# A fused attention and two expert layers on one core: weight slots, residues and the beginning rearranged

## The chip, the core and the metric

The kernel runs on one core of a Trainium2 chip. The engines named are TensorE (PE in the rows; PEld its weight loads), VectorE (DVE), ScalarE (ACT), GpSimd (POOL) and SyncE (SP), which issues nearly all DMAs. The metric is device time in microseconds; lower is better. Times are from one launch of the whole program.

## The reference

Attention over 2 batches of 8 heads, 768 positions of 64 values, in which a score counts only where the 6-bit hash of query and key agree; then two layers of 1536 tokens, 512 wide, 2048 in the middle.

```python
q_bits = einsum(q, proj) > 0 ; k_bits = einsum(k, proj) > 0     # 6 bits
mask = q_bucket == k_bucket
scores = where(mask, q @ k.T / 8, -1e9)
attn = softmax(scores) ; out = attn @ v                          # per head
x = heads side by side                                           # 1536 x 512
h = x @ w_in ;  g = h * tanh(softplus(h)) ;  x = g @ w_out       # layer 1
h = x @ w_in2 ; g = P(h) / (Q(|h|) + 1e-6) ; out = g @ w_out2    # layer 2, P cubic, Q quadratic
```

The weights arrive as 64-bit floats. Matmuls run on 32-bit floats rounded for TensorE, so each operand is split into a rounded part (`hi`) and a residue (`lo`), and a product is three matmuls: hi·hi, hi·lo and lo·hi.

## The kernel before

**Attention.** The order of the work is written by hand: a table `order` (line 510) gives each operation its step, six steps for a head, and `slot_ops` emits the operations of a step in the table's order. Every engine works through its own queue in that order. In a step of head h TensorE computes the scores `sp` of one block of 128 keys (`st`, line 346) and the matmuls `mp` of one block of a later head (`smax`, 313); VectorE reduces `mp` to its maxima `m` (line 324), ScalarE takes the exponential `e` of `sp` (358). `sp`, `mp` and a small tile of `vsum` share one pool of three PSUM tiles, so a new tile waits for the `e` or `m` that reads an older one. Other steps add `pv` and `dn`, the products of `e` with the values and with ones (two blocks at once in step 5, the sixth step), and `codes`, the hash matmuls `cp`. `cp` and `dn` take turns in a single PSUM bank, which `code_k` (VectorE, 297) and `code_q` (ScalarE, 306) must have read before it comes free.

For each head, `hi` (ScalarE) rounds key and query into `qB`, `lo` takes the residue `qX`: on GpSimd (line 67), for head 0 on VectorE (line 70). SP then moves rows between tiles: `move_k` (230), `move_x` (236), `move_h` (240). `code_q` writes rows of `qB` that `move_k` reads. `fin_a` turns six maxima into a row (`smt`, then `stt`, line 333), and `fin_b` (339) writes it into `qB` by two DMAs from SP and two from GpSimd.

A list `start` (574) gives the first operations by hand, up to the scores of head 0.

**Weights.** A layer has 16 slots (128 columns of `w_in`, 128 rows of `w_out`, each as hi and lo). During attention, ten slots of layer 1 are loaded in halves (`ring_load`) and converted from 64-bit to 32-bit by three VectorE operations (lines 100, 103, 106; "bits"). Slots 0 to 4 are split into hi and lo on GpSimd (a few residues on VectorE) and stored to DRAM (`ring_split`), then loaded into their tiles (`first`); slots 5 to 9 are stored as 32-bit floats. Tiles 0 to 2 of the weights' pool also hold the raw heads that `load` fetches.

**Layers.** `moe` runs iterations i, one slot and one block of 512 tokens each. An iteration issues `gl` (VectorE's residue of the activation of i-1, in `back`), 12 matmuls `h` (`gemm1`), the activation on ScalarE (`front`), and 12 matmuls `y` of i-1 (`gemm2`), whose last four need `gl`. Beside the first block, slots 5 to 9 are loaded as floats and split, and slots 10 to 15 are converted from the 64-bit source in four pieces each through a ring of five tiles: `direct_load`, `direct_bits` in one iteration, `direct_hi` and `direct_lo` in the next. `tail` (593) emits what is left of attention's last heads in iterations 1, 2 and 4.

Of the kernel before, what the change touches and what calls it, by code (L numbers as in the profile page):

```python
# [9 lines left out]
F32 = mybir.dt.float32  # L10
# [10 lines left out]
NF = DFF // 128  # L21
# [6 lines left out]
NBITS = 6  # L28
EARLY, FIRST = 5, (84, 68, 76, 52, 60)
SPLIT1, HERE1, W_AT, W_LEAD = 5, 10, (3, 9, 15, 17, 21), 4  # L30
DVE_LO = (("lo", 0),)
ENG = dict(
    lo="pp", hi="aa", xhi="a", xlo="dd", whi="pppp", wlo="pdpp",
)
C_AT = 16
ROW, TINY = 31, 2.0 ** -60
C1_AT = 2, 14
RING, EP, GB = (2, 5), 4, 2
# [6 lines left out]
def attention_moe_moe(ctx: ExitStack, tc: tile.TileContext, kq, v, proj2, cst, eye, w1, w2, ab, out):  # L45
# [115 lines left out]
    def attention(actx, tctx):  # L161
# [22 lines left out]
        VF = [v_p.tile([128, NC, 2, D], F32, tag=f"vf{i}", name=f"vf{i}") for i in range(2)]  # L184
        ones = v_p.tile([128, 32], F32, tag="ones", name="ones")

        def memsets():
            nc.gpsimd.memset(cs_t, 0.0)
# [6 lines left out]
            nc.gpsimd.memset(ones, 1.0)  # L195
            nc.gpsimd.memset(bias[:, 1:2], 1.000001)
# [73 lines left out]
        def qhalf(t, a):  # L270
            return t[:, a * HALF:(a + 1) * HALF]
# [15 lines left out]
        def codes(h):  # L287
            if not 0 <= h < B * H:
                return
            ct[h] = pvp.tile([128, 512], F32, tag="dn", name="cp")  # L290
            both(ct[h], p_raw, raws[h], start=True, stop=True)

        def code_k(h):
            if not 0 <= h < B * H:
                return
            for a in range(2):
                nc.vector.tensor_scalar(  # L297
                    out=qhalf(KK[h % 4][0:32, 0], a), in0=ct[h][64 * a:64 * a + 32, 0:HALF],
                    scalar1=cs_t[:, 1:2], scalar2=cs_t[:, 2:3], op0=ALU.is_gt, op1=ALU.mult,
                )  # L300

        def code_q(h):
            if not 0 <= h < B * H:
                return
            for a in range(2):
                nc.scalar.activation(
                    out=qhalf(qB[h % 4], a)[0:32], in_=ct[h][64 * a + 32:64 * a + 64, 0:HALF],
                    func=ACT.Sign, bias=cs_t[:, 0:1],
                )
# [164 lines left out]
        nh = B * H  # L474
        parts = [(f, s) for f in range(HERE1 if wide64 else 0) for s in range(PARTS[0])]
        jobs = {}

        def ring_out(l, f, s):
            (ring_split if f < SPLIT1 else ring_store)(l, f, s)

# [4 lines left out]
        for n, p in enumerate(parts):  # L485
            i = n // 5 * 24 + W_AT[n % 5]
            for fn, d in ((ring_load, -W_LEAD), (convert, 0), (ring_out, 1)):
                jobs.setdefault(max(0, i + d), []).append((fn, p))
# [8 lines left out]
        def first(f, n):  # L497
            if wide64:
# [33 lines left out]
            ("xlo", xlo, 24, 0),
            ("vred", vred, -5, 0),
            ("move_x", move_x, -14, 1),
            ("move_h", move_h, -12, 1),
            ("load", load, -31, 1),
# [7 lines left out]
        for name, fn, at, per in order:  # L544
# [29 lines left out]
        start = (
            ("load", 0), ("get", 0), ("get", 1), ("hi", 0), ("codes", 0), ("khi", 0, 0), ("lo", 0), ("load", 1),
            ("code_q", 0), ("code_k", 0), ("khi", 0, 1), ("get", 2), ("move_x", 0), ("smax", 0, 0), ("hi", 1),
            ("smax", 0, 1), ("move_k", 1), ("load", 2), ("lo", 1), ("smax", 0, 2), ("codes", 1), ("move_h", 0),
            ("smax", 0, 3), ("smax", 0, 4), ("smax", 0, 5), ("fin_a", 0), ("fin_b", 0), ("code_k", 1), ("code_q", 1),
            ("load_v", 0), ("move_x", 1), ("load", 3), ("hi", 2), ("move_k", 2), ("smax", 1, 0), ("coef",),
            ("move_h", 1), ("smax", 1, 1),  # L580
        )
# [17 lines left out]
    def moe(mctx, tctx, tail):  # L599
# [114 lines left out]
        def run():  # L714
# [72 lines left out]
            for i in range(-5, len(seq) + 5):  # L787
# [99 lines left out]
```

## Time and profile before

| | us |
|---|---|
| median of 3 runs | 808.4 (806.15 to 809.41) |
| the profiled execution, its own time | 807.36 |
| its span, first to last instruction | 805.3 |
| PE busy | 772.7 (96%) |
| DVE busy | 593.8 (74%) |
| ACT busy | 422.4 (52%) |
| POOL busy | 83.2 (10%) |

All times in rows count from the first instruction of the span. A row of the timeline gives start, duration, engine, line, operation, out<-in with shapes, and how many alike were merged; in brackets the engine's idle time ahead of it and what ended it. PE's duration of a matmul includes the way through its pipeline, so that neighbours overlap. The first `h` of the layers starts at 276.1 us.

### The profile page before, as it was taken

Reading aid. Unit: us, or ns where it says so; the run is one execution under the profiler, and the core shown is the slowest. Engines: PE = TensorE matmul, PEld = TensorE weight load, DVE = VectorE, ACT = ScalarE, POOL = GpSimd, SP = SyncE. Lnnn points to the kernel's source line nnn. Section 1 sums busy time; section 2 is a strip of 40 time slices with the busy share of each in tenths; the row PEclk is TensorE's granted clock in tenths of the full one; section 3 lists DMA queues with packets and bytes.
Section 4 is the critical chain, followed back from the end, with each engine's and each line's share of the span. In section 5 each row is a group of like instructions: output and inputs, shape, how many; then the busy total and the mean of one; then the engine's idle time right before and its main releaser. Section 6 shows DMA issues by size and latency. Waiting matters only on the chain.

```text
span 805.3 us, 10855 instructions
## 1 busy us (share of the span) xinstructions
PE 772.7 (96%) x3744; PEld 571.0 (71%) x3744; DVE 593.8 (74%) x1067; ACT 422.4 (52%) x682; POOL 83.2 (10%) x104
## 2 busy tenths in 40 slices
PE   4799999999999999999999999999999999999997
PEld 2455455555555587888888888887888888888886
DVE  5667878878766367656554667739998988888885
ACT  3345454655555554323122324358787777677664
POOL 3332442531221000000000000000000000000000
PEclk8899999999999999999999999999999999999999
DMA  4757466766765462334454487730000100001001
GB/s 112 211 162 200 147 171 197 211 167 191 223 182 145 123 209 79 105 105 150 157 168 141 138 261 256 221 115 2 1 1 0 53 1 0 1 15 39 0 1 52
DMA packets 60629, 94.91 MB, mean 118 GB/s; under 512 B 20896, under 2 KB 29088, under 8 KB 60576
## 3 DMA queue, kind: packets, MB, share of 16 engines
q1 hardware_dynamic: 59552, 94.21, 39.6%
q8 instruction: 29, 0.48, 0.2%
q14 instruction: 24, 0.20, 0.1%
q0 software_dynamic: 1024, 0.03, 0.1%
HBM read 62.43 MB, written 19.45 MB: 102 GB/s over the span
## 4 chain that ended last, share of the span: by engine, by line
PE 82%; DVE 9%; DMA 5%; ACT 2%; issue 1%; SPq 1%; DVEq 0%; ACTq 0%
PE h L632 30%; PE y L652 16%; PE y L650 14%; PE pv L276 7%; PE sp L353 6%; PE dn L379 4%; PE mp L320 4%; DVE m L324 3%; DMA r<-w 2%; DMA kk<-qX 1%; DVE w L70 1%; DVE t L103 1%; DMA kk<-qB 1%; DVE kk L297 1%; DVE r L106 1%
## 5 line engine op out<-in xcount | busy, mean ns | idle before, releaser
L632 PE MATMUL h<-xh,w 128*128 128x512 f32 x768 | 204.9, 389 | 0.0
L632 PEld LDWEIGHTS h<-xh,w 128*128 128x128 f32 x768 | 144.1, 188 | 30.6 <-issue 0.6
L324 DVE TENSOR_REDUCE m<-mp 128x1 f32<-128x768 f32 x96 | 90.7, 952 | 44.8 <-PE mp L320 44.4
L70 DVE TENSOR_TENSOR gl<-ep,gh 128x512 fp32r<-128x512 f32 x96 | 65.9, 687 | 64.9 <-ACT ep L676 64.2
L358 ACT ACTIVATE e<-sp 128x768 f32<-128x768 f32 x96 | 76.0, 810 | 65.1 <-PE sp L353 63.8
L675 ACT ACTIVATE gh<-h 128x512 fp32r<-128x512 f32 x48 | 28.7, 598 | 147.6 <-PE h L632 138.8
L632 PE MATMUL h<-xl,w 128*128 128x512 f32 x384 | 102.6, 389 | 0.0
L652 PE MATMUL y<-w,gh 128*128 128x512 f32 x384 | 96.3, 389 | 0.0
L650 PE MATMUL y<-gh,w 128*128 128x512 f32 x384 | 94.8, 389 | 0.0
L632 PEld LDWEIGHTS h<-xl,w 128*128 128x128 f32 x384 | 72.1, 188 | 15.0
L650 PEld LDWEIGHTS y<-gh,w 128*128 128x128 f32 x384 | 72.1, 188 | 15.0
L652 PEld LDWEIGHTS y<-w,gh 128*128 128x128 f32 x384 | 72.1, 188 | 15.0
L320 PE MATMUL mp<-kk,qB 128*128 128x384 f32 x192 | 54.7, 374 | 22.8 <-DVE m L324 11.7
L276 PE MATMUL pv<-e,vf 128*64 128x384 f32 x384 | 73.8, 506 | 0.0
L320 PEld LDWEIGHTS mp<-kk,qB 128*128 128x128 f32 x192 | 34.8, 199 | 33.2 <-DVE m L324 16.7
L353 PE MATMUL sp<-qB,kk 128*128 128x384 f32 x192 | 55.8, 371 | 0.6 <-ACT e L358 0.6
L682 ACT ACTIVATE ep<-h 128x512 f32<-128x512 f32 x48 | 28.6, 595 | 52.4 <-PE h L632 52.4
L353 PEld LDWEIGHTS sp<-qB,kk 128*128 128x128 f32 x192 | 31.2, 190 | 33.9 <-issue 17.2
L106 DVE SCALAR_TENSOR_TENSOR r<-r,t 128x256 int32<-128x256 int32 (+1 forms) x108 | 51.2, 474 | 4.6 <-DMA w<-r 0.5
L103 DVE SCALAR_TENSOR_TENSOR t<-r,t 128x256 int32<-128x256 int32 (+1 forms) x108 | 51.7, 479 | 3.7
L652 PE MATMUL y<-w,gl 128*128 128x512 f32 x192 | 53.3, 392 | 0.5 <-DVE gl L70 0.4
L684 DVE TENSOR_TENSOR n<-n,ep 128x512 f32<-128x512 f32 x48 | 33.1, 690 | 26.8 <-ACT n L683 26.8
(72 smaller groups left out, 1037.8 us busy)
## 6 DMA issues: line engine op xcount, KB each, us to landing
r<-w SPq DMA_DIRECT2D x88, 256.0 KB
w<-w SPq DMA_DIRECT2D x21, 512.0 KB
r<-w SPq DMA_DIRECT2D x20, 512.0 KB
w<-r SPq DMA_DIRECT2D x64, 128.0 KB
w<-r SPq DMA_DIRECT2D x30, 256.0 KB
kq<-kq SPq DMA_DIRECT2D x16, 384.0 KB
kk<-qB SPq DMA_DIRECT2D x15, 384.0 KB
w<-w SPq DMA_DIRECT2D x20, 256.0 KB
```

The source lines that it names most:

```text
L70: nc.vector.tensor_tensor(out=o, in0=i, in1=f32(h), op=ALU.subtract)
L103: lambda: nc.vector.scalar_tensor_tensor(out=t, in0=r[:, :, 1], scalar=-0x40000000, in1=t, op0=ALU.bitwise_and, op1=ALU.bitwise_or),
L106: lambda: nc.vector.scalar_tensor_tensor(out=o, in0=r[:, :, 0], scalar=29, in1=t, op0=ALU.logical_shift_right, op1=ALU.bitwise_or),
L276: nc.tensor.matmul(out=o[64 * a:64 * a + 64, 0:HALF], lhsT=w, rhs=qhalf(x, a), start=start, stop=stop)
L320: nc.tensor.matmul(out=p[:, a, 0:HALF], lhsT=qB[h % 4][:, c * 128:(c + 1) * 128], rhs=qhalf(KK[h % 4][:, 0], a), start=True, stop=True,)
L324: nc.vector.tensor_reduce(out=mt[h][:, c:c + 1], in_=halves(p), op=ALU.max, axis=AX.XY)
L353: nc.tensor.matmul(out=p[:, a, 0:HALF], lhsT=kk[:, c * 128:(c + 1) * 128], rhs=qq[:, a * HALF:(a + 1) * HALF], start=(i == 0), stop=(i == 1),)
L358: nc.scalar.activation(out=wide(e), in_=halves(p), func=ACT.Exp, scale=1.0 / D ** 0.5)
L632: nc.tensor.matmul(out=p, lhsT=w[:, c * 128:(c + 1) * 128], rhs=x[:, c, :], start=(n == 0), stop=(n == 11))
L650: nc.tensor.matmul(out=y[m], lhsT=w[:, DM + m * 128:DM + (m + 1) * 128], rhs=g, **s)
L652: nc.tensor.matmul(out=y[m], lhsT=g[:, m * 128:(m + 1) * 128], rhs=w[:, DM:2 * DM], **s)
L684: nc.vector.tensor_tensor(out=v_, in0=v_, in1=u, op=ALU.mult)
```

## The change

- Seven weight slots (`EARLY = 7`) are converted during attention, one half in each head, at steps 7, 13, 19, ... Slots 0 to 2 (`SHARED = 3`) go through DRAM as before; slots 3 to 6 are split by GpSimd straight into their tiles (`slot_split`). Nothing is stored as 32-bit floats for layer 1 any more. All residues of weights in attention are GpSimd's.
- Nine slots, 7 to 15, are converted beside layer 1's first block in four pieces each, from iteration 1 on (it was six, from iteration 2); hi and residue are taken in the iteration of the bits.
- The residues `lo` of all heads are VectorE's.
- Other steps: `hi`, `move_k`, `lo`, `code_q`, `norm`, `xlo`, `vred`, `move_x`, `move_h`; the maxima of heads 1 and 2 are spread over later steps.
- Another `start`: three loads of heads first; the codes of head 0 are computed twice, into a second PSUM tile for ScalarE; 28 calls of `warm`, a matmul of ones by ones of 128 columns into that tile; the maxima of head 0 are taken between residues of heads 1 and 2.

```diff
-EARLY, FIRST = 5, (84, 68, 76, 52, 60)
-SPLIT1, HERE1, W_AT, W_LEAD = 5, 10, (3, 9, 15, 17, 21), 4
+EARLY, SHARED, FIRST = 7, 3, (78, 66, 72, 60, 60, 60, 60)
+W_AT, W_LEAD = 7, 4
 ENG = dict(
-    lo="pp", hi="aa", xhi="a", xlo="dd", whi="pppp", wlo="pdpp",
+    lo="dd", hi="aa", xhi="a", xlo="dd", whi="pppp", wlo="pppp",
 )
-C1_AT = 2, 14
+C1_AT = 1, 14
...
+    def slot_split(l, f, s):
+        w = raw.pop((l, f, s)).bitcast(F32)[:, 0:CH[l]]
+        if (l, f) not in W:
+            slot(l, f, lambda f: wpool)
+        h = W[l, f][:, 0, part(l, s)]
+        hi_of("whi", f)(h, w)
+        lo_of("wlo", f)(W[l, f][:, 1, part(l, s)], w, h)
...
-            ct[h] = pvp.tile([128, 512], F32, tag="dn", name="cp")
-            both(ct[h], p_raw, raws[h], start=True, stop=True)
+            ct[h] = [pvp.tile([128, 512], F32, tag="dn", name="cp")] * 2
+            if h == 0:
+                ct[h][1] = warm_up[0]
+            for t in ct[h][0:1 + (h == 0)]:
+                both(t, p_raw, raws[h], start=True, stop=True)
+        def warm(n):
+            if not warm_up:
+                warm_up.append(pvp.tile([128, 512], F32, tag="pv", name="wm"))
+            for _ in range(n):
+                nc.tensor.matmul(out=warm_up[0][0:32, HALF:512], lhsT=ones, rhs=wones, start=True, stop=True)
...
-            (ring_split if f < SPLIT1 else ring_store)(l, f, s)
+            ring_split(l, f, s) if f < SHARED else slot_split(l, f, s)
...
-            i = n // 5 * 24 + W_AT[n % 5]
+            i = W_AT + 6 * n
...
-            ("hi", hi, -18, 1),
-            ("move_k", move_k, -17, 1),
-            ("lo", lo, -18, 1),
+            ("hi", hi, -16, 1),
+            ("move_k", move_k, -15, 1),
+            ("lo", lo, -15, 1),
...
-            ("code_q", code_q, -15, 1),
+            ("code_q", code_q, -14, 1),
...
-                todo = [(c // 2 if h == 1 else at + 6 * h + c, (h, c)) for h in range(nh) for c in range(per)]
+                todo = [((at, c - 2, 4 + c)[h] if h < 3 else at + 6 * h + c, (h, c)) for h in range(nh) for c in range(per)]
...
+            ("load", 0), ("get", 0), ("get", 1), ("load", 1), ("load", 2), ("warm", 5), ("hi", 0), ("codes", 0),
+            ("khi", 0, 0), ("lo", 0), ("warm", 5), ("code_k", 0), ("code_q", 0), ("hi", 1), ("khi", 0, 1), ("get", 2),
+            ("move_k", 1), ("lo", 1), ("move_x", 0), ("smax", 0, 0), ("warm", 2), ("smax", 0, 1), ("warm", 2), ("hi", 2),
...
-                        at(i + 1, direct_hi, f, s)
-                        at(i + 1, direct_lo, f, s)
-                        at(spread(n - RING[1], C1_AT, NF - HERE1) + 1 if n >= RING[1] else -1, direct_load, f, s)
+                        at(i, direct_hi, f, s)
+                        at(i, direct_lo, f, s)
+                        at(spread(n - RING[1], C1_AT, NF - EARLY) if n >= RING[1] else -1, direct_load, f, s)
```

SP's queue in the beginning, before. `kk_130<-qB_122` is `move_k` of head 3, the two `qB_120<-stt_118` are `fin_b` of head 1, `kq` the load of a head.

```order
L230 DMA kk_129<-qB_121 64x2x768
L240 DMA qX_124<-qB_120 64x768
L236 DMA kk_129<-qX_125 64x768
L240 DMA qX_125<-qB_121 64x768
L205 DMA kq<-kq 128x768 x2
L119 DMA r<-w 128x1024
L230 DMA kk_130<-qB_122 64x2x768
L339 DMA qB_120<-stt_118 1x6x32 x2
L211 DMA vf_132<-v 128x12x64
```

The same stretch of SP's queue now.

```order
L251 DMA qX_124<-qB_120 64x768
L247 DMA kk_129<-qX_125 64x768
L216 DMA kq<-kq 128x768 x2
L251 DMA qX_125<-qB_121 64x768
L222 DMA vf_132<-v 128x12x64
L362 DMA qB_120<-stt_118 1x6x32 x2
L241 DMA kk_130<-qB_122 64x2x768
L119 DMA r<-w 128x1024
```

`move_k` of head 3 has come from ahead of head 1's `fin_b` to behind it.

VectorE's queue in a head in the middle, before: from a `fin_a` (`smt`, `stt`) on, with a conversion of a half of weights (L100 to L106) behind `code_k` (L297).

```order
L330 TENSOR_SCALAR smt1_116<-m_1004 128x6
L333 STREAM_TRANSPOSE stt1_118<-smt1_116 128x32
L324 TENSOR_REDUCE m_1158<-mp_1191 128x1
L297 TENSOR_SCALAR kk1_128<-cp_1195,cst_114 32x384 x2
L324 TENSOR_REDUCE m_1158<-mp_1211 128x1
L268 TENSOR_SCALAR vsc_1223<-vsp_1220 128x2
L100 TENSOR_SCALAR t_1227<-r_1131 128x512
L103 SCALAR_TENSOR_TENSOR t_1227<-r_1131,t_1227 128x512
L106 SCALAR_TENSOR_TENSOR r_1131<-r_1131,t_1227 128x512
L324 TENSOR_REDUCE m_1158<-mp_1238 128x1
```

The same of VectorE now, for the same head.

```order
L353 TENSOR_SCALAR smt1_116<-m_1018 128x6
L356 STREAM_TRANSPOSE stt1_118<-smt1_116 128x32
L100 TENSOR_SCALAR t_1189<-r_1090 128x512
L103 SCALAR_TENSOR_TENSOR t_1189<-r_1090,t_1189 128x512
L106 SCALAR_TENSOR_TENSOR r_1090<-r_1090,t_1189 128x512
L347 TENSOR_REDUCE m_1165<-mp_1200 128x1
L320 TENSOR_SCALAR kk1_128<-cp_1205,cst_114 32x384 x2
L347 TENSOR_REDUCE m_1165<-mp_1225 128x1
L70 TENSOR_TENSOR qX1_124<-kq_843,qB1_120 128x768
L279 TENSOR_SCALAR vsc_1239<-vsp_1236 128x2
```

The conversion has moved two reductions ahead, and the residue `qX` stands where it was.

VectorE's queue in one iteration of layer 1, before: from one `gl` to the next, two pieces (`r`) and the residues of a slot in floats (`w8`) and of two pieces of the iteration before.

```order
L70 TENSOR_TENSOR gl_2886<-ep_2854,gh_2855 128x512
L100 TENSOR_SCALAR t_2884<-r_2818 128x256
L103 SCALAR_TENSOR_TENSOR t_2884<-r_2818,t_2884 128x256
L106 SCALAR_TENSOR_TENSOR r_2818<-r_2818,t_2884 128x256
L100 TENSOR_SCALAR t_2885<-r_2868 128x256
L103 SCALAR_TENSOR_TENSOR t_2885<-r_2868,t_2885 128x256
L106 SCALAR_TENSOR_TENSOR r_2868<-r_2868,t_2885 128x256
L70 TENSOR_TENSOR w8_2703<-w8_2703 128x512 x2
L70 TENSOR_TENSOR w11_2838<-r_2757,w11_2838 128x256
L70 TENSOR_TENSOR w11_2838<-r_2816,w11_2838 128x256
L70 TENSOR_TENSOR gl_2937<-ep_2905,gh_2906 128x512
```

An iteration of VectorE now, from one `gl` to the next (neither shown): three pieces, bits and residues.

```order
L100 TENSOR_SCALAR t_2725<-r_2648 128x256
L103 SCALAR_TENSOR_TENSOR t_2725<-r_2648,t_2725 128x256
L106 SCALAR_TENSOR_TENSOR r_2648<-r_2648,t_2725 128x256
L100 TENSOR_SCALAR t_2726<-r_2650 128x256
L103 SCALAR_TENSOR_TENSOR t_2726<-r_2650,t_2726 128x256
L106 SCALAR_TENSOR_TENSOR r_2650<-r_2650,t_2726 128x256
L100 TENSOR_SCALAR t_2727<-r_2707 128x256
L103 SCALAR_TENSOR_TENSOR t_2727<-r_2707,t_2727 128x256
L106 SCALAR_TENSOR_TENSOR r_2707<-r_2707,t_2727 128x256
L70 TENSOR_TENSOR w8_2700<-r_2648,w8_2700 128x256
L70 TENSOR_TENSOR w8_2700<-r_2650,w8_2700 128x256
L70 TENSOR_TENSOR w9_2758<-r_2707,w9_2758 128x256
```

The residues of the pieces now belong to the bits of the same iteration.

## Rows read from the trace of the kernel before

**Rows 1.** Stretches: window, PE, PEld, DVE, ACT, POOL busy, clock, DMA share, GB/s.

```profile
20.00:58.00 38.00, 32.34 (x174) 18.18 (x173) 25.38 (x38) 16.05 (x23) 14.95 (x17) 0.93 0.68 181
58.00:276.00 218.00, 207.12 (x1242) 115.23 (x1242) 159.50 (x274) 115.56 (x173) 60.95 (x69) 0.99 0.64 181
```

**Rows 2.** PE's waits: total us, times, longest.

```profile
PE mp L320 <- DVE m L324: 11.7, 12, 1.9
```

**Rows 3.** Timeline of PE: start, duration, operation, idle time ahead.

```profile
4.08 1.55 PE L276 MATMUL cp<-kq,pr 128*64 128x384 f32 x4 [4.08 <-DMA pr<-proj]
...
19.23 0.84 PE L353 MATMUL sp<-qB,kk 128*128 128x384 f32 x2
...
27.48 0.62 PE L320 MATMUL mp<-kk,qB 128*128 128x384 f32 x2 [3.66 <-ACT qB L306]
...
86.88 0.90 PE L320 MATMUL mp<-kk,qB 128*128 128x384 f32 x2 [1.88 <-DVE m L324]
87.72 2.83 PE L276 MATMUL pv<-e,vf 128*64 128x384 f32 x8
...
97.81 0.87 PE L276 MATMUL cp<-kq,pr 128*64 128x384 f32 x4
```

**Rows 4.** Timeline of the beginning: `hi` of head 1, transpose of head 0.

```profile
7.86 0.84 ACT L61 ACTIVATE qB<-kq 128x768 fp32r<-128x768 f32 x1
...
15.54 0.21 DVE L333 STREAM_TRANSPOSE stt<-smt 128x32 f32<-128x32 f32 x1
```

**Rows 5.** Timeline of one head in the middle, all engines.

```profile
124.80 0.51 PE L353 MATMUL sp<-qB,kk 128*128 128x384 f32 x2
...
126.05 1.51 PE L276 MATMUL pv<-e,vf 128*64 128x384 f32 x8
...
129.79 1.55 SPq L339 DMA_DIRECT2D qB<-stt  x2
...
131.52 0.68 SPq L230 DMA_DIRECT2D kk<-qB  x1
...
133.77 0.42 DVE L100 TENSOR_SCALAR t<-r 128x512 int32<-128x512 int32 x1
...
135.36 1.16 ACT L306 ACTIVATE qB<-cp,cst 32x384 fp32r<-32x384 f32 x2 [3.13 <-DMA kk<-qB]
...
135.62 0.95 DVE L324 TENSOR_REDUCE m<-mp 128x1 f32<-128x768 f32 x1
...
136.62 0.62 PE L320 MATMUL mp<-kk,qB 128*128 128x384 f32 x2 [1.08 <-DVE m L324]
```

**Rows 6.** Groups by line: count, busy us, mean ns of one, idle before.

```profile
L70 DVE TENSOR_TENSOR qX<-kq,qB 128x768 fp32r<-128x768 f32 x1 | 1.0, 958 | 4.7 <-ACT qB L61 4.7
...
L426 DVE TENSOR_SCALAR z<-rc 24x32 f32<-24x32 f32 x16 | 6.6, 413 | 0.5
...
L429 DVE TENSOR_SCALAR rc<-rc 24x32 f32<-24x32 f32 x16 | 2.7, 170 | 0.5
...
L67 POOL TENSOR_TENSOR r<-r 128x512 fp32r<-128x512 f32 x8 | 10.3, 1293 | 0.7
```

**Rows 7.** Timeline of VectorE in layer 1, and one wait of PE.

```profile
284.55 0.29 DVE L100 TENSOR_SCALAR t<-r 128x256 int32<-128x256 int32 x1 [0.87 <-DMA r<-w]
...
302.09 0.76 DVE L70 TENSOR_TENSOR w<-r,w 128x256 fp32r<-128x256 f32 x2
302.76 0.68 DVE L70 TENSOR_TENSOR gl<-ep,gh 128x512 fp32r<-128x512 f32 x1
...
304.15 0.42 DVE L106 SCALAR_TENSOR_TENSOR r<-r,t 128x256 int32<-128x256 int32 x1
305.85 0.30 DVE L100 TENSOR_SCALAR t<-r 128x256 int32<-128x256 int32 x1 [1.28 <-DMA r<-w]
...
322.21 1.20 PE L650 MATMUL y<-gl,w 128*128 128x512 f32 x4 [0.49 <-DVE gl L70]
```

**Rows 8.** Chain that ended last, in order of time: start, us, what.

```profile
323.41 2.72 PE h L632 x12
```

More of the change, by code (lines that the diff above doesn't have):

```diff
@@ L185, in attention @@
         ones = v_p.tile([128, 32], F32, tag="ones", name="ones")
+        wones = v_p.tile([128, 128], F32, tag="wones", name="wones")
         def memsets():
+            nc.vector.memset(ones, 1.0)
+            nc.vector.memset(wones, 1.0)
             nc.gpsimd.memset(cs_t, 0.0)
@@ L194, in memsets @@
                 nc.gpsimd.memset(f32(SM[i]), 0.0)
-            nc.gpsimd.memset(ones, 1.0)
             nc.gpsimd.memset(bias[:, 1:2], 1.000001)
@@ L289, in codes @@
                 return
-            ct[h] = pvp.tile([128, 512], F32, tag="dn", name="cp")
-            both(ct[h], p_raw, raws[h], start=True, stop=True)
+            ct[h] = [pvp.tile([128, 512], F32, tag="dn", name="cp")] * 2
[3 more added lines that the diff above has]
+                both(t, p_raw, raws[h], start=True, stop=True)
+        warm_up = []
+        def warm(n):
[3 more added lines that the diff above has]
+                nc.tensor.matmul(out=warm_up[0][0:32, HALF:512], lhsT=ones, rhs=wones, start=True, stop=True)
         def code_k(h):
@@ L297, in code_k @@
                 nc.vector.tensor_scalar(
-                    out=qhalf(KK[h % 4][0:32, 0], a), in0=ct[h][64 * a:64 * a + 32, 0:HALF],
+                    out=qhalf(KK[h % 4][0:32, 0], a), in0=ct[h][0][64 * a:64 * a + 32, 0:HALF],
                     scalar1=cs_t[:, 1:2], scalar2=cs_t[:, 2:3], op0=ALU.is_gt, op1=ALU.mult,
@@ L306, in code_q @@
                 nc.scalar.activation(
-                    out=qhalf(qB[h % 4], a)[0:32], in_=ct[h][64 * a + 32:64 * a + 64, 0:HALF],
+                    out=qhalf(qB[h % 4], a)[0:32], in_=ct[h][1][64 * a + 32:64 * a + 64, 0:HALF],
                     func=ACT.Sign, bias=cs_t[:, 0:1],
@@ L474, in attention @@
         nh = B * H
-        parts = [(f, s) for f in range(HERE1 if wide64 else 0) for s in range(PARTS[0])]
+        parts = [(f, s) for f in range(EARLY if wide64 else 0) for s in range(PARTS[0])]
         jobs = {}
         def ring_out(l, f, s):
-            (ring_split if f < SPLIT1 else ring_store)(l, f, s)
+            ring_split(l, f, s) if f < SHARED else slot_split(l, f, s)
         def convert(l, f, s):
@@ L497, in first @@
         def first(f, n):
-            if wide64:
+            if wide64 and f >= SHARED:
+                pass
+            elif wide64:
                 if n == 0:
@@ L529, in attention @@
             ("spread", spread, 12, 1),
-            ("norm", norm, 22, 0),
+            ("norm", norm, 23, 0),
             ("xhi", xhi, 23, 0),
[L532 to L535, printed above, removed]
+            ("xlo", xlo, 29, 0),
+            ("vred", vred, -6, 0),
+            ("move_x", move_x, -13, 1),
+            ("move_h", move_h, -11, 1),
             ("load", load, -31, 1),
@@ L549, in attention @@
             elif name == "smax":
-                todo = [(c // 2 if h == 1 else at + 6 * h + c, (h, c)) for h in range(nh) for c in range(per)]
+                todo = [((at, c - 2, 4 + c)[h] if h < 3 else at + 6 * h + c, (h, c)) for h in range(nh) for c in range(per)]
             elif name.startswith("fin_"):
-                todo = [(at + 6 * h + (h == 1), (h,)) for h in range(nh)]
+                todo = [((at, 3, 9)[h] if h < 3 else at + 6 * h, (h,)) for h in range(nh)]
             elif per > 0:
@@ L574, in attention @@
         start = (
[L575 to L580, printed above, removed]
+            ("load", 0), ("get", 0), ("get", 1), ("load", 1), ("load", 2), ("warm", 5), ("hi", 0), ("codes", 0),
+            ("khi", 0, 0), ("lo", 0), ("warm", 5), ("code_k", 0), ("code_q", 0), ("hi", 1), ("khi", 0, 1), ("get", 2),
+            ("move_k", 1), ("lo", 1), ("move_x", 0), ("smax", 0, 0), ("warm", 2), ("smax", 0, 1), ("warm", 2), ("hi", 2),
+            ("smax", 0, 2), ("warm", 2), ("move_k", 2), ("lo", 2), ("move_h", 0), ("smax", 0, 3), ("warm", 2),
+            ("smax", 0, 4), ("warm", 2), ("smax", 0, 5), ("codes", 1), ("fin_a", 0), ("fin_b", 0), ("code_q", 1),
+            ("code_k", 1), ("load_v", 0), ("move_x", 1), ("load", 3), ("warm", 8), ("smax", 1, 0), ("smax", 1, 1),
+            ("move_h", 1), ("coef",),
         )
@@ L587, in run @@
             for name, *k in start:
+                if name == "warm":
+                    warm(*k)
+                    continue
                 done.add(("move_k" if name == "khi" else name, tuple(k[:1]) if name == "khi" else tuple(k)))
@@ L761, in run @@
             for f in range(EARLY, NF):
-                if wide64 and f < SPLIT1:
-                    at(-1, slot_both, 0, f, wp)
-                elif wide64 and f >= HERE1:
+                if wide64:
                     for s in range(PARTS[1]):
-                        n = PARTS[1] * (f - HERE1) + s
-                        i = spread(n, C1_AT, NF - HERE1)
+                        n = PARTS[1] * (f - EARLY) + s
+                        i = spread(n, C1_AT, NF - EARLY)
                         at(i, direct_bits, f, s)
-                        at(i + 1, direct_hi, f, s)
-                        at(i + 1, direct_lo, f, s)
-                        at(spread(n - RING[1], C1_AT, NF - HERE1) + 1 if n >= RING[1] else -1, direct_load, f, s)
+                        at(i, direct_hi, f, s)
+                        at(i, direct_lo, f, s)
+                        at(spread(n - RING[1], C1_AT, NF - EARLY) if n >= RING[1] else -1, direct_load, f, s)
                 else:
@@ L796, in run @@
                 for fn, k in now:
-                    if fn in (slot_hi, direct_hi):
+                    if fn is slot_hi:
                         fn(*k)
@@ L805, in run @@
                     o()
+                for fn, k in now:
+                    if fn is direct_hi:
+                        fn(*k)
                 if i >= 0:
```

## The prediction, made before the changed kernel ran

> **What bounds the kernel now.** I read the stretches first, then TensorE's waits, then the timeline of those waits. From 276 us on TensorE has no room: it is the layers' matmuls back to back. The attention ahead of it has room: between 58 and 276 us TensorE is busy 207.12 of 218 us, so 10.88 us idle at a mean granted clock of 0.99, and between 20 and 58 us 32.34 of 38 us, so 5.66 us idle at a mean of 0.93 [rows 1]. Twelve of the waits are for the reduction `m` on VectorE, 11.7 us together [rows 2]. The reader is to see in [rows 3] what such a wait is and what it can drag behind it: the first codes run 1.55 us at 4.08, the same four matmuls 0.87 us at 97.81, nearly twice as long, as the lower of its two levels (1.2 against 2.4 GHz) makes it; after the 1.88 us of idle time at 86.88 the eight `pv` take 2.83 us, and 1.51 us at 126.05 where nothing was idle.
>
> One head in the middle shows the cause [rows 5]. VectorE converts a piece of weights from 133.77 to the reduction at 135.62, 1.85 us; that reduction ends at 136.57 and TensorE, which needs its PSUM tile, sat 1.08 us until 136.62. In the same head ScalarE's `code_q` stands 3.13 us behind the copy `move_k`: issued at 131.52, right behind the 1.55 us of `fin_b` on SP, landed by 135.36, 3.84 us later.
>
> **The middle (58 to 276 us).** The change puts the conversion two steps earlier, into the step with most matmuls after it (`pv`, a third of `dn`), and `code_q` one step later. What VectorE has to do hardly changes: some 12 residues of 0.958 us come to it there [rows 6], 11.5 us, and about five conversions of 1.85 us leave, 9.3 us; so 159.5 us [rows 1] become 162 of 207, 78%. A step of `sp` and `mp` lasts 1.25 us (124.80 to 126.05) [rows 5], with `pv` 1.51 more and with the long `dn` as much again, and a whole head some 15 us, its steps at 0, 1.2, 4.7, 6.7, 9.4 and 10.6. With `sp` and `mp` ahead, 0.95 us each and the other work of the step behind them, the reductions end at 2.1, 3.2, 6.7, 9.1, 11.7 and 13.8 us; a score matmul needs the reduction of two steps before, and those stand at 4.7, 6.7, 9.4, 10.6, 14.7 and 15.9 us. No reduction is last any more. To be gained are the 10.88 us and the slow clock, 0.01 of 207 us, about 1.8: 12.7 us. What is late next is `dn`, since it takes the PSUM bank that `code_q` must have read: by steps `code_q` ends at 12.3 us, in heads with two stores on SP ahead of `move_k` at 12.8, and `dn` stands at 13.3. With a cover of 0.5 to 1 us I leave 1.7 us for heads where SP is later. Bounds: 0 left over, or all 10.88 us in another place. Taken: **11.0 us off**.
>
> A rule of the Trainium skill speaks against this step. The row: `z`, 24x32, takes 413 ns in the mean, the next operation on the same shape 170 [rows 6], so something holds it up. The page "SBUF — State Buffer", section "SBUF: two separate sides", says that VectorE with two SBUF inputs and GpSimd lock one port pair, and the loser waits out the other's whole instruction. The residue has two SBUF inputs and GpSimd's weight residue lasts 1.29 us [rows 6]: by the rule 12 times 1.29 us more, VectorE at 86%, still under TensorE; the sum stays, and the third rival below would have a chance of 0.22 by it.
>
> **The beginning (0 to 58 us).** Before, `stt` of head 0 ends at 15.75 and its scores start at 19.23, 3.5 us later [rows 3, 4]. After: the second copy of the codes ends near 4.08 + 2 x 1.55 = 7.2; `code_q` (1.16) to 8.5, `hi` of head 1 (0.84 [rows 4]) to 9.4; VectorE's residue of head 1 to 10.4, six reductions of 0.95 and the residue of head 2 to 17.0, `fin_a` 0.4: 17.4, and 3.3 to 3.5 us on, 20.7. So 1.5 us later. The warm matmuls add nothing to the path while TensorE waits anyway; without that cover they are 28 calls of 128 columns, about 4 us at the pace of the two 384-column calls (four matmuls) in 0.87 us.
>
> By the Trainium skill, "TensorE: Matmul & The Clock Gate", section "What's actually happening", the engine starts throttled and activity releases it; [rows 3] agree at 4.08. If the first five warm matmuls did it, the codes would save 0.68 us each copy and the sum would be 1.4 us lower; I count nothing, since TensorE is idle again before the codes.
>
> Then two waits arise that were not there. In the rows of order, SP issued `move_k` of head 3 ahead of head 1's `fin_b`, and now behind it, and `code_q` is a step later. From the end of `mp` of the last block of head 1: reduction 0.95, `fin_a` 0.4, `fin_b` 1.55, landing 3.84, `code_q` 1.16, together 7.9 us; TensorE has till `dn` two `pv`, two steps, `vsum`: 1.51 x 2 + 1.25 x 2 + 0.4 = 5.9. So `dn` of head 0 waits 2 us, and 0.4 more as VectorE is late. One head on the same, with a second reduction ahead and no `vsum`: 8.9 against 5.5, 3.4 us. Behind `dn` on TensorE everything stands, as it is in order. A load (head 3) and ScalarE's queue cost another 1.3 us, and after the longer wait the clock falls once, as at 86.88: 1.4 to 1.8 us. Lost: 2.4 + 3.4 + 1.3 + 1.6 = 8.7 us. Before, the same stretch lost 5.66 us and, at clock 0.93, 2.3 us: 8.0, among it the 3.66 us at 27.48 [rows 1, 3]. So 0.7 us and the 1.5 us: 2.2 us; the bounds go from 6 us on (the clock falls three times) to 4 us off (both waits covered). The new waits being worked out and the cover being not, I take **1.5 us on**.
>
> **Layer 1 (from 276 us).** Nine slots of four pieces are converted beside the matmuls, where it was six slots and ten halves of others already in float. A piece costs VectorE 1.2 us of bits (`gl` at 302.76 to the end of bits at 304.57 is 1.81, `gl` 0.61 of it) and 0.36 of residue (two in 0.76) [rows 7]. Three pieces and `gl`: 5.3 us of the 5.44 us that an iteration lasts (two groups of twelve matmuls, 2.72 us each [rows 8]). It fits, without slack. The wait for a load in each iteration, 1.28 us at 305.85 [rows 7], goes: the residue is taken in the same iteration, so that two pieces stand ready instead of one, and the third comes 4 us after its ring tile is free against about 3.7 us that a load needed. But two iterations carry attention's last heads: in the first, `recip` and `xl`, 2.3 us on top, with the first data not there before 5.8 us after the layer starts (it was 8.5, behind a double-size load that is gone [rows 7]); `gl` is then 0.8 us late. In the fifth, norm and `xl` with ScalarE between, 2.5 us less 0.5 of slack: 2.0 us. The 0.49 us at 322.21 [rows 7] was such a wait and goes. Bounds: 0.5 us off if the data come early, 6 us on if the first data come at 8.5 us as before. Taken: **2.3 us on**.
>
> **Sum.** 11.0 - 1.5 - 2.3 = 7.2 us off the profiled execution of 807.36 us (span 805.3 and 2.1 around it): 800.2 us. The median of the runs shown lies 1.0 us above that execution; inside their spread I take a third of it: 800.5 us. Nothing else in the layers moves.
>
> **Rivals.** (1) The beginning works as well: `move_k` lands before `dn` needs it, the clock stays up. For it: matmuls put just where TensorE idled. Against: the order of SP. Then 5.5 us more come off: 795 us. (2) Slower: VectorE bounds layer 1. If the idle time for a load stays, as 1.28 us at 305.85, an iteration needs 5.3 + 1.3 = 6.6 us, 1.15 us over, 15 us in 13 iterations; less the 5 us of slack that `gl` has at the start, but with the two tail iterations on top 15 to 20 us: 813 us or more. It decides from about 1.1 us of idle time for each iteration on. For it: 5.3 of 5.44. Against: two ready pieces in the ring. (3) The change does not do what it says: the wait of each head moves, from `mp` to `dn` or to the residue. Then 10.9 of the 12.7 us stay, and one clock fall less: 808 us. For it: the thin cover at `dn`. Against: the table of steps.
>
> **Chances.** Forecast 0.50 (own range 794 to 806), (1) 0.20, (2) 0.13, (3) 0.17. Less than 0.5%, 4 us, cannot be told from no change on this kernel. Faster than 804.4: 0.42 + 0.20 + 0.02 + 0.03 = 0.67. Same: 0.07 + 0.03 + 0.12 = 0.22; slower: 0.01 + 0.08 + 0.02 = 0.11. The range of 790 to 809 takes in (1) and (3) and leaves (2).
>
> **What would show it.** Middle: no wait for `m` between 60 and 230 us; each head near 15.1 us, 16 before. Beginning: scores of head 0 at 20 to 21 us; two waits of `dn` for `code_q`, 2 to 4 us, near 35 and 52 us. Layer 1: waits for `gl` in the second and fifth iterations, no VectorE wait for loads after the first. I am wrong if TensorE still idles some 0.8 us in each head, or if the layer loses time in every iteration.

## The result: slower, and the profile after

The changed kernel takes 818.05 us in the median (816.0 to 820.27) against 807.7 for the kernel before on the same chip: ratio 1.0133 [1.0114, 1.0152], 10.4 us slower. The forecast was 800.5 us, its range ended at 809. The span of the profiled execution is 817.6 us, 12.3 more than before.

First the waits of TensorE in the changed kernel (total us, times, longest), then those of ScalarE for the copy of k:

```profile
PE dn L402 <- ACT qB L329: 22.0, 11, 4.0
PE y L679 <- DVE gl L70: 1.6, 1, 1.6
PE sp L376 <- DMA qB<-stt: 1.1, 1, 1.1
PE mp L343 <- DVE m L347: 0.4, 1, 0.4
```

```profile
ACT qB L329 <- DMA kk<-qB: 29.6, 9, 4.9
```

The 11.7 us of `mp` for `m` [rows 2] are gone: 0.4. In their place stand 22.0 us of `dn` for `code_q`, 6.0 of them in the beginning (two waits), 16.0 in nine heads of the middle, and behind that wait `code_q`'s own, for `move_k`'s transfer. The same stretches, and TensorE's timeline:

```profile
20.00:58.00 38.00, 32.50 (x161) 19.23 (x161) 24.67 (x39) 14.32 (x20) 9.10 (x14) 0.91 0.53 139
58.00:276.00 218.00, 199.46 (x1182) 111.36 (x1184) 145.63 (x261) 114.74 (x167) 52.35 (x70) 0.98 0.53 141
...
80.90:83.60 2.70, 2.70 (x16) 0.58 (x16) 0.00 (x0) 0.77 (x1) 0.00 (x0) 0.50 0.41 141
```

```profile
21.95 0.59 PE L376 MATMUL sp<-qB,kk 128*128 128x384 f32 x2 [1.07 <-DMA qB<-stt]
...
38.99 2.23 PE L402 MATMUL dn<-e,ones 128*32 128x384 f32 x16 [2.02 <-ACT qB L329]
...
60.54 2.79 PE L402 MATMUL dn<-e,ones 128*32 128x384 f32 x16 [3.97 <-ACT qB L329]
...
69.27 0.87 PE L287 MATMUL cp<-kq,pr 128*64 128x384 f32 x4
...
80.89 2.79 PE L402 MATMUL dn<-e,ones 128*32 128x384 f32 x16 [3.66 <-ACT qB L329]
...
157.97 0.87 PE L287 MATMUL cp<-kq,pr 128*64 128x384 f32 x4
172.70 0.87 PE L287 MATMUL cp<-kq,pr 128*64 128x384 f32 x4
...
287.43 1.19 PE L661 MATMUL h<-xh,w 128*128 128x512 f32 x4
...
318.61 1.21 PE L679 MATMUL y<-gl,w 128*128 128x512 f32 x4 [1.64 <-DVE gl L70]
```

What to see: TensorE does 199.5 us of work from 58 to 276 us instead of 207.1 [rows 1]. A head without a wait lasts 14.73 us (157.97 to 172.70). After three of the waits (3.97, 3.66 and 2.87 us) the clock is granted at half, the 1.2 GHz level, and the sixteen `dn` take 2.79 us instead of 1.50; after two others of like length (2.60 us at 115.35, 3.20 at 246.46) they take 1.50. Layer 1 starts at 287.43 instead of 276.1, 11.3 us late; from there to the end it is 1.0 us longer than before.

Why `dn` waits, in one head of the changed kernel: SP, ScalarE and TensorE.

```profile
69.48 1.16 SPq L436 DMA_DIRECT2D cs<-dv  x2
69.85 0.85 ACT L61 ACTIVATE qB<-kq 128x768 fp32r<-128x768 f32 x1
70.68 0.70 SPq L222 DMA_DIRECT2D vf<-v  x1
71.48 0.78 SPq L138 DMA_DIRECT2D w<-r  x1
72.36 0.37 SPq L139 DMA_DIRECT2D w<-r  x1
72.90 0.66 SPq L241 DMA_DIRECT2D kk<-qB  x1
...
79.68 1.16 ACT L329 ACTIVATE qB<-cp,cst 32x384 fp32r<-32x384 f32 x2 [4.57 <-DMA kk<-qB]
80.89 0.87 PE L402 MATMUL dn<-e,ones 128*32 128x384 f32 x4 [3.66 <-ACT qB L329]
```

`hi` ends at 70.70, `move_k` (L241) is issued at 72.90, behind a load of v and two stores of a weight half, and lands only in time for `code_q` at 79.68; `dn`, which needs the bank that `code_q` reads, could have started at 77.2. In before `move_k` stood right behind `fin_b` (129.79 and 131.52 [rows 5]) and landed 3.84 us after its issue. The chain that ended last holds this transfer nine times in the changed kernel. Three of them, the first with neither load nor store just ahead of it on SP, the others behind a load of v and two stores:

```profile
55.50 3.74 DMA kk<-qB
...
72.90 6.69 DMA kk<-qB
...
142.06 5.87 DMA kk<-qB
```

### The profile page after: what moved, and what is told of

Its sections match the earlier page's. It is cut to its first block, busy times and chain, and to the rows that moved or that the text cites. A ratio compares the mean times of both kernels' runs of the same rounds, so it can differ in the third digit from the quotient of the medians.

```text
span 817.6 us, 10933 instructions
## 1 busy us (share of the span) xinstructions
PE 784.3 (96%) x3804; PEld 577.2 (71%) x3804; DVE 593.8 (73%) x1102; ACT 424.9 (52%) x684; POOL 65.4 (8%) x98
## 3 DMA queue, kind: packets, MB, share of 16 engines
HBM read 57.71 MB, written 14.73 MB: 89 GB/s over the span
## 4 chain that ended last, share of the span: by engine, by line
PE 84%; DMA 6%; DVE 4%; ACT 3%; issue 1%; SPq 1%; POOL 0%; ACTq 0%; DVEq 0%
PE h L661 29%; PE y L681 16%; PE y L679 14%; PE sp L376 8%; DMA kk<-qB 6%; PE pv L287 5%; PE dn L402 5%; PE mp L343 4%; PE cp L287 2%; ACT qB L329 2%; PE wm L314 1%; DVE t L103 1%; DVE w L70 1%; DVE r L106 1%; DVE t L100 0%
## 5 line engine op out<-in xcount | busy, mean ns | idle before, releaser
L661 PEld LDWEIGHTS h<-xh,w 128*128 128x128 f32 x768 | 144.1, 188 | 30.6 <-issue 0.6
L381 ACT ACTIVATE e<-sp 128x768 f32<-128x768 f32 x96 | 77.2, 811 | 73.6 <-PE sp L376 73.2
L402 PE MATMUL dn<-e,ones 128*32 128x384 f32 x384 | 42.2, 547 | 22.0 <-ACT qB L329 22.0
L106 DVE SCALAR_TENSOR_TENSOR r<-r,t 128x256 int32<-128x256 int32 (+1 forms) x114 | 52.2, 458 | 4.7
L679 PE MATMUL y<-gl,w 128*128 128x512 f32 x192 | 51.6, 390 | 1.6 <-DVE gl L70 1.6
```

The lines of the kernel that those rows point to most:

```text
L106: lambda: nc.vector.scalar_tensor_tensor(out=o, in0=r[:, :, 0], scalar=29, in1=t, op0=ALU.logical_shift_right, op1=ALU.bitwise_or),
L381: nc.scalar.activation(out=wide(e), in_=halves(p), func=ACT.Exp, scale=1.0 / D ** 0.5)
L402: nc.tensor.matmul(out=pvt[h, "d"][32 * n:32 * n + 32, 0:HALF], lhsT=ones, rhs=qhalf(pt[h, c - 1 + n // 2], n % 2), start=(c == 1), stop=( ...
L661: nc.tensor.matmul(out=p, lhsT=w[:, c * 128:(c + 1) * 128], rhs=x[:, c, :], start=(n == 0), stop=(n == 11))
L679: nc.tensor.matmul(out=y[m], lhsT=w[:, DM + m * 128:DM + (m + 1) * 128], rhs=g, **s)
```

## Experiments

Theory A: the place of `hi` and `move_k` makes `dn` wait. Rivals: transfers share the queues, wherever `move_k` stands (B); VectorE, which got the residues, is late (C).

**The three entries as before (e1).**

```diff
-            ("hi", hi, -16, 1),
-            ("move_k", move_k, -15, 1),
+            ("hi", hi, -18, 1),
+            ("move_k", move_k, -17, 1),
...
-            ("code_q", code_q, -14, 1),
+            ("code_q", code_q, -15, 1),
```

> The kernel after, with three entries of the table as they were before: hi at -18 (was -16), move_k at -17 (was -15), code_q at -15 (was -14). On SP move_k then stands right behind fin_b, ahead of the gather and of the two stores of a converted slot half. Theory A (the new stall is move_k's place: its transfer is issued 3.5 to 5.7 us behind fin_b, behind the stores, so code_q and with it dn come late): the 22.0 us in 11 waits of dn for code_q fall to under 4 us, the three or four slow-clock dn calls (2.79 us) go, layer 1 starts near 265 us instead of 287.4, and the time is 792 to 800. Rival B (the transfer is long because other transfers share the queues, whatever its place): waits of dn of 10 us or more stay, 808 or more. Rival C (VectorE, which got the residues, is late and holds code_k, cp and the maxima): waits of mp for m come back, some 10 us, 803 to 810.

800.02 us (0.9927 [0.9904, 0.995] of before), 18 us less than the changed kernel. No wait of `dn` is left, so B falls as far as it says "wherever `move_k` stands". Waits for `m` came back, but small (the rows are of an execution of 804.62 us, the slowest of seven):

```profile
PE mp L343 <- DVE m L347: 7.1, 18, 0.9
PE cp L287 <- ACT qB L329: 2.7, 1, 2.7
```

ScalarE is held here too: `code_q`, a step earlier than in the changed kernel, waits for the residue `qX` in twelve heads, 20.7 us in all. This residue does not stand where it was, as the section on the change has it: before, it was GpSimd's, three steps earlier.

**The copy ahead of `fin_b` (e5).**

```diff
-            ("hi", hi, -16, 1),
-            ("move_k", move_k, -15, 1),
+            ("hi", hi, -18, 1),
+            ("move_k", move_k, -18, 1),
```

> The kernel after, with hi and move_k both at -18 and code_q left at -14: the copy of k is issued ahead of fin_b, some 5 us earlier in each head than in the kernel after. Theory A: no wait of dn over 0.5 us is left, the beginning's two waits (2.0 and 4.0 us) go too; layer 1 starts near 262 us, and the time is 790 to 796. Rival B (transfers share the queues: it now stands right behind the 384 KB load of kq): flight of 5 to 7 us, but with three steps more time, so waits of 0 to 3 us in single heads; 795 to 803. Rival C (VectorE): 803 or more with waits of mp for m.

794.77 us (0.9849 [0.9825, 0.9872]). As A said; all engines, slots and layer 1 are the changed kernel's. `code_q` hardly waits for anything, TensorE from 58 to 230 us is 169.73 us busy of 172, against 156.66 in the changed kernel:

```profile
PE cp L287 <- ACT qB L329: 2.5, 1, 2.5
PE mp L343 <- DVE m L347: 2.3, 6, 0.5
```

```profile
58.00:230.00 172.00, 169.73 (x1016) 95.65 (x1012) 133.93 (x237) 97.91 (x146) 48.69 (x66) 1.00 0.60 161
```

**Only the stores behind the copy (e2):** `W_AT` 9 instead of 7.

> The kernel after, with W_AT = 9 instead of 7: loading, converting and storing a weight half come two steps later in each head, so that on SP the two stores stand behind move_k; hi, move_k and code_q stay where they are. Theory A in the form 'the stores ahead of move_k are what makes it late' (they wait for GpSimd's residue, and their 512 KB are in flight ahead of it): move_k lands 3.8 us after its issue, the waits of dn from 80 us on (16.0 us in 9 waits) fall to under 5 us; the two at 39 and 60 us (6.0 us), where there is no store ahead, stay; 800 to 806. If hi's place on ScalarE is what makes it late (it ends 3.5 us behind fin_b): most waits stay, 811 to 817. Rival C (VectorE): waits stay or grow, since the conversion now stands nearer to the reductions; 815 to 822.

811.91 us (1.006 [1.0039, 1.0081]), 6 us less: by its time in the range of the second expectation, by its waits near the first. The waits of `dn` from 62 us on fell from 16.0 to 5.5 us (0.3 to 0.4 in most heads, 1.24 and 2.38 in two late ones); the two of the beginning, 2.25 and 4.35, stayed; but waits for `m` came, 3.8 us in 6, I take it because the conversion now stands nearer to the reductions. So the stores are a good part of the waits; that the place of `hi` and `move_k` is all of the rest is not shown by this run alone.

**Residues on GpSimd again (e4):** `lo="pp"`.

> The kernel after, with the residues of q and k on GpSimd again (1.82 us each instead of 0.95 on VectorE), at the same step. Theory A: dn waits for move_k and code_q, which do not read the residue; the waits of dn stay near 22 us or grow a little, since GpSimd ends the weight residue later and the stores stand ahead of move_k: 817 to 824. Rival C (VectorE is overloaded by the residues): dn's waits shrink by half or more, 805 to 811.

815.71 us (1.0107 [1.0077, 1.0138]); 22.2 us of `dn` for `code_q` in 11, as in the changed kernel. C falls, though the time is a little under the 817 to 824 expected. The 2 us less lie in the beginning: scores of head 0 at 20.06 us instead of 21.95.

**The same in e5 (e7):** e5 with `lo="pp"`.

> The kernel with hi and move_k both at -18 (794.8 us), with the residues of q and k on GpSimd again (1.82 us against 0.95 on VectorE), at the same step. If the residues' engine is what gains in the middle (it was the reason given for VectorE's better order): waits of mp for m or of sp for the second half of k come back, 800 or more. If the place of hi and move_k is all of it: TensorE's waits between 58 and 262 us stay under 4 us, as now (2.3 us for m and 0.5 for e), and the time is 792 to 797.

797.79 us (0.9879 [0.9858, 0.99]), 3 us over e5 and 0.8 over what I expected. In the middle nothing changes (2.3 us for `m`, 0.5 for `e`); the 3 us lie ahead of 60 us, where two waits of `dn` are back (0.40 and 1.94).

**One number in the kernel before (e10).**

```diff
-            ("move_k", move_k, -17, 1),
+            ("move_k", move_k, -18, 1),
```

> The kernel before, with one entry changed: move_k at -18 (was -17), so that it is issued ahead of fin_b instead of behind it. In before, code_q holds ScalarE for 1.7 to 4.0 us in each head until move_k has landed, and mp waits 1 us for m. If that wait of mp comes from ScalarE's hold (scores and maxima share three PSUM tiles, so a late exp makes a late tile): the waits of mp for m (11.7 us in 12) and for qB (8.2 us in 2, part of it) go, 796 to 801, and the whole gain of the middle was to be had by this one number. If the wait comes from VectorE's conversions (bits of 1.8 us ahead of the reduction): it stays, 805 to 808.

797.28 us (0.9879 [0.9857, 0.9901]): 10.6 us off the kernel before, by one entry. Waits of ScalarE for the copy before, and then TensorE's and ScalarE's in e10:

```profile
ACT qB L306 <- DMA kk<-qB: 28.2, 11, 4.0
```

```profile
PE mp L320 <- DVE m L324: 1.1, 2, 0.6
...
ACT qB L306 <- DMA kk<-qB: 0.8, 2, 0.6
```

```profile
58.00:262.00 204.00, 200.10 (x1205) 112.58 (x1203) 156.52 (x273) 115.74 (x171) 61.09 (x69) 1.00 0.69 193
```

VectorE has the old conversions and is busy for 156.5 of 204 us, and `mp` hardly waits for `m` any more. So the wait that the prediction wanted to remove hung on the late copy too, which held ScalarE. In the kernel before, the head of [rows 5] shows how:

```profile
133.52 0.60 PE L353 MATMUL sp<-qB,kk 128*128 128x384 f32 x2
...
134.31 0.52 PE L320 MATMUL mp<-kk,qB 128*128 128x384 f32 x2
...
134.68 0.52 PE L353 MATMUL sp<-qB,kk 128*128 128x384 f32 x2
...
136.55 1.51 ACT L358 ACTIVATE e<-sp 128x768 f32<-128x768 f32 x2
```

When TensorE wants a tile for the next `mp`, all three are taken: two hold scores, whose exponentials run only from 136.55 on, behind the late `code_q`, and the third holds the `mp` of 134.31, whose reduction stands behind the conversion and ends at 136.57. The late copy and the conversion were both needed for the wait. One thing stays open: which of the three tiles a `mp` gets is settled when the program is built. In ten heads of the kernel before, the `mp` ahead of the long `dn` gets back the tile of the `mp` before it, as here; in e10 in two. So I can't say how much of the 10.6 us is ScalarE's hold itself and how much this choice.

**The late steps in the kernel before (e11):** `hi`, `move_k`, `lo`, `code_q`, `move_x`, `move_h` at the steps of the changed kernel.

> The kernel before with six offsets of the table as they are after: hi -16, move_k -15, lo -15, code_q -14, move_x -13, move_h -11; its engines, slots, beginning and layer 1 stay. If the place of hi and move_k is what made the changed kernel slow, this alone must make the kernel before slow: waits of dn for code_q of 15 to 25 us, 815 to 825. If it needed another part (the residues on VectorE, seven slots, the beginning), it stays within 806 to 810.

814.29 us (1.0083 [1.0057, 1.011]), a little under the expected 815 to 825. It takes no other part of the change to make the kernel slow:

```profile
PE dn L379 <- ACT qB L306: 16.7, 9, 4.5
```

**The beginning (e9, e13, e14) and the tail (e8, e12), all on e5.** e9 issues the load of head 3 ahead of `move_k` of head 2.

> The kernel with hi and move_k both at -18 (794.8 us), with the load of head 3 issued earlier in the list of the beginning, ahead of move_k of head 2. There cp of head 3 waits 2.53 us at 27.93 for code_q of head 2, which stands on ScalarE behind hi of head 3, which waits 3.87 us for that load. Expected: hi of head 3 no longer waits, the 2.5 us go, and with them the slow clock behind (pv 2.18 for six at 30.57); 791 to 793. If the bus is the limit in the beginning (0.46 to 0.65 of the DMA engines busy), v and the copies of k land later, and 1 us or nothing is left: 793.5 to 796.

794.05 us, 0.7 under e5, which is within the error: the 791 to 793 expected was missed. The wait of 2.53 us is gone, but layer 1 starts only 1.1 us earlier (261.45, 262.53); in this execution the scores of head 0 came 1.05 us later (21.24).

e13 is e9 without the 28 `warm` calls.

> The kernel with hi and move_k at -18 and the load of head 3 early (794.05 us), without the 28 warm matmuls of the beginning. If they hold TensorE's clock up: without them the first cp, maxima and scores run at the 1.2 GHz level (cp 1.55, mp 0.98 for two instead of 0.62), but VectorE's reductions of 0.95 us pace the maxima of head 0 anyway; I expect the scores of head 0 up to 1 us later and one or two slow stretches more between 20 and 35 us, 794.5 to 796.5. If the clock of the beginning hides behind VectorE altogether, or the warm matmuls stand in the way of the path: 792.5 to 794.3.

793.49 us, no clear difference to e9. Rows of e13, then of e9:

```profile
7.74 2.26 PE L343 MATMUL mp<-kk,qB 128*128 128x384 f32 x6 [0.76 <-ACT qB L329]
...
19.84 0.98 PE L376 MATMUL sp<-qB,kk 128*128 128x384 f32 x2 [0.54 <-DMA qB<-stt]
```

```profile
21.24 0.98 PE L376 MATMUL sp<-qB,kk 128*128 128x384 f32 x2 [1.08 <-DMA qB<-stt]
```

From the first `mp` to the scores of head 0 it is 12.1 us in both (7.74 to 19.84, 9.12 to 21.24), so VectorE's reductions pace the maxima at either speed of TensorE; and two `sp` take 0.98 us in both where the scores start. What the `warm` calls do cost shows ahead of the maxima. `code_q` of head 0 reads the PSUM tile into which they write, and starts behind the last of them; first the changed kernel, then e13:

```profile
9.18 1.18 ACT L329 ACTIVATE qB<-wm,cst 32x384 fp32r<-32x384 f32 x2 [3.68 <-PE wm L314]
```

```profile
7.07 1.18 ACT L329 ACTIVATE qB<-wm,cst 32x384 fp32r<-32x384 f32 x2 [1.50 <-PE wm L287]
```

That is 2.1 us here, 1.4 in e9 (8.45) and 0.4 in e5 (7.42), as ten `warm` matmuls took 2.27, 1.53 and 1.28 us in these executions. In e13 layer 1 starts 1.5 us earlier than in e9, and a second stall in the layer (0.94 us) takes a part of it back.

e12 moves the last pair's norm, `xh` and `xl` from the fifth iteration of layer 1 to the sixth.

> The kernel with hi and move_k at -18 and the load of head 3 early (794.05 us), with the last pair's norm, xh and xl put into the sixth iteration of layer 1 instead of the fifth; the fifth has three pieces to convert, the sixth two. My reading of the one stall in layer 1 (1.62 us of gl): three pieces, norm and xl in one iteration. With one piece less (1.56 us of VectorE) it shrinks to 0.3 us or nothing: 792.5 to 793.2. If ScalarE's xh ahead of gh is the cause, 0.5 to 1 us stays: 793.3 to 794.

792.26 us (0.9815 [0.9789, 0.9841]), the fastest run here but for e14. TensorE's one wait for `gl` in layer 1, in e9 and then in e12:

```profile
292.78 1.21 PE L679 MATMUL y<-gl,w 128*128 128x512 f32 x4 [1.62 <-DVE gl L70]
```

```profile
276.09 1.20 PE L679 MATMUL y<-gl,w 128*128 128x512 f32 x4 [0.84 <-DVE gl L70]
```

They are not the same stall. The layer starts at 261.45 in e9 and at 262.26 in e12, so the first lies 31.3 us behind its start and the second 13.8. The stall of the fifth iteration is gone, though ScalarE's `xh` still stands ahead of `gh`: the first expectation held. The 0.84 us belong to the second iteration, for which the prediction forecast 0.8; e13 has that stall too (0.94 us, beside 1.64 in the fifth) and e14 0.27 us of it.

e14 is e12 with the residues of heads 1 and 2 behind `fin_a` of head 0; they are then taken after `code_q` has written into `qB`, so these residues are other values than the reference needs, though they cost the same operations.

> The kernel of the sixth-iteration tail, with the residues of heads 1 and 2 behind fin_a of head 0 in VectorE's order of the beginning instead of between its reductions. In the traces one of them (0.95 us) stands between the reductions of head 0, the other ahead of them: the scores of head 0 start 1 to 1.9 us earlier, 20.2 to 19.3 instead of 21.2, and the time is 0.8 to 1.8 us under the kernel of the sixth-iteration tail. If the reductions are paced by TensorE's clock or by the loads of kq, nothing is gained; if head 1's maxima then come late, mp or cp waits near 28 us and it is 0.5 to 1 us longer.

791.27 us, 1.0 us less than e12. Scores of head 0 come at 20.52 instead of 22.04; half of that lies ahead of the first `mp` (9.15 and 9.91), which differs between executions. From there to the scores it is 11.4 us instead of 12.1, so in the beginning VectorE's order does set the start, by some 0.75 us, under the 1 to 1.9 expected.

e8 puts `xl` of every second pair on GpSimd.

> The kernel with hi and move_k both at -18 (794.8 us), with the residue xl of every second pair of heads, the last among them, on GpSimd, which has no work after attention. My reading of the stall in layer 1 is that two iterations carry attention's last heads on VectorE: the one stall of 1.58 us (gl, fifth iteration) then loses VectorE's 1.22 us of xl and shrinks to some 0.8 us, since ScalarE's xh (0.94 us ahead of gh) stays; 794.0, within the error of no change. If xl is read late from GpSimd, the first matmuls of the blocks that read it wait: 796 or more. If the stall is the conversion itself (rival 2: VectorE bounds the layer), it stays at 1.6 us, 794.8.

794.82 us, no change; the stall stayed at 1.54 us, for another reason than the three that I had. VectorE's `gl` began 1.1 us earlier behind the layer's start than in e9 (29.5 and 30.6 us), but took 1.06 us longer beside GpSimd's `xl`:

```profile
292.83 2.15 POOL L67 TENSOR_TENSOR xl<-xf,xh 128x256 fp32r<-128x256 f32 x2 [45.61 <-ACT xh L61]
...
293.78 1.75 DVE L70 TENSOR_TENSOR gl<-ep,gh 128x512 fp32r<-128x512 f32 x1
...
298.73 0.69 DVE L70 TENSOR_TENSOR gl<-ep,gh 128x512 fp32r<-128x512 f32 x1
```

## Why the prediction was wrong, step by step

**The middle: 11.0 us off predicted, 5.8 on measured** (from `cp` of the sixth head, 63.73 before and 69.27 after, to the start of layer 1: 212.4 and 218.2). This step failed, in the sentence that `code_q` ends at 12.3 or 12.8 us of a head, `dn` stands at 13.3, and "with a cover of 0.5 to 1 us I leave 1.7 us". Its first half held: no wait for `m` in the middle, and 14.7 us for a free head where 15.1 was forecast. The second did not. I gave `move_k` the flight of the old place, 3.84 us, and its issue no delay but the two stores', 0.5 us. That is right only where SP has neither load nor store to issue just ahead of it: in two heads `dn` waits for nothing, and `code_q` ends 0.85 us before it (164.54 and 165.39 in one of them), the cover that I had. With a load of v ahead `dn` waits 0.5 and 0.7 us, with two stores 0.3 and 0.9, with both 2.6, 2.9 and 3.7; in two late heads, with loads of finished weights ahead, 1.3 and 3.2. The copy is then issued up to 2.7 us after `hi` has ended, since SP issues those others first (in the whole middle it waited for GpSimd's residue 0.8 us), and it lands after 4 to 6.7 us. That makes nine waits, 16.0 us, and two falls of the clock to half (80.89 and 149.23, 1.29 us each): 18.6 us where 1.7 were left for it. The difference of 16.9 us accounts for the 16.8 by which the term was off.

Behind it lies half a reading: I took 11.7 us of `mp` for `m` as VectorE's load alone, because the row names `m`. The 28.2 us that ScalarE waited for the copy stood in that trace, and one of them (3.13 us) in [rows 5]; e10 shows that moving the copy alone takes nearly all the waits for `m` away, with the conversions where they were. The change moved exactly this copy, and to the wrong side.

**The beginning: 1.5 on predicted, 5.5 on measured** (69.27 against 63.73), inside its bounds. Scores of head 0 are 2.7 us later, where 1.5 was worked out. A term put at nothing failed there, that the warm matmuls "add nothing to the path": `code_q` starts behind them at 9.18, where the sum had it near 7.2 and e13 without them has 7.07. The two waits of `dn`, 2.02 and 3.97 us, were forecast with 2.4 and 3.4. Mis-sized was what they drag along: the clock fell in both (2.23 and 2.79 us for sixteen `dn`). From the scores of head 0 to the sixth `cp` it is 2.8 us more than before, where 0.7 was the sum: 1.2 us of idle time (6.88 against 5.66), and 1.6 us for the same 209 matmuls (40.44 against 38.84, at a mean granted clock of 0.89 against 0.93). The 0.7 us that I took off for a cover did not come. The first warm matmuls did not speed up the codes either: the first `cp` takes 1.55 us as in [rows 3], so the 1.4 us that the Trainium skill's rule ("TensorE: Matmul & The Clock Gate", section "What's actually happening") would have given did not come (in e5's execution the second copy of the codes took 0.83 us, the first 1.49).

**Layer 1: 2.3 on predicted, 1.0 on measured.** The stall came in the fifth iteration (1.64 for 2.0 us); the one forecast for the second did not come in this execution, as VectorE's `gl` there was in time; its first data arrived 5.5 us after the layer's start (292.95), where not before 5.8 was worked out. In e12, e13 and e14 it came. Behind those data VectorE waits for no load here, so rival 2 is out.

**The rivals.** The third was the right one in kind (the wait moves from `mp` to `dn`), and wrong in price: 808 us took over the old 10.9 us, while the new waits of the middle are 16.0 us and bring 2.6 us of slow clock of their own. Rival 1 is what the kernel does once the copy is early, which the change did not do: 794.8 us in e5, where it said 795, and near it term by term. The middle is 10.4 us off (11.0 forecast), the beginning 3.2 off (4.0), layer 1 1.0 on (2.3). The Trainium skill's rule of the shared ports ("SBUF — State Buffer", section "SBUF: two separate sides") did not bear on the middle: the residue takes 945 ns in the mean in the changed kernel, as the single one before [rows 6]. VectorE's work there fell, from 156.4 to 143.6 us, where 2.5 more were worked out: six conversions left instead of five, and `xl` of 128x256 takes 405 ns in the mean instead of 1351. That did not decide the time.

## What to carry to other kernels

A wait that a trace puts down to one engine may also hang on a third one that keeps the shared resource: ask which engine in that stretch waits longest and for what, before pricing the row that is named. When a step is moved, price its DMA anew at the new place: what SP has ahead of it, what each of those waits for, and what is then on the way with it. Where a wait is that of a single transfer, try moving just this transfer; here one number in the table gave 10.6 us, and the whole change with the copy early 12.8. When a stall has shrunk, look whether it is still the same one.

## What the runs showed of the hardware

The same copy of 384 KB landed 3.74 us after its issue with neither load nor store issued just ahead of it, after 4.0 and 4.6 us behind two stores, and after 5.6 to 6.7 us behind a load and two stores. TensorE's granted clock fell to half after waits of 2.87, 3.66 and 3.97 us, and not after others of 2.60 and 3.20. A two-input operation of VectorE, `gl`, took 1.75 us instead of 0.69 beside a two-input operation of GpSimd, and ended 0.55 us after it (295.53, 294.98). The Trainium skill says in "SBUF — State Buffer", section "SBUF: two separate sides", that such operations lock one port pair and the loser waits out the other's instruction; this run agrees.
